# Raw weight pieces placed in the next chunk's tiles, a store cut in two, and loads moved to ScalarE's queue, in a kernel of attention, Fourier mixing and routed experts

## The chip, the cores and the metric

The kernel runs on one core of one Trainium2 chip. The metric is the device time of one launch in microseconds (us). Engines are TensorE (PE, with its weight loads as PEld), VectorE (DVE), ScalarE (ACT), GpSimd (POOL) and SyncE (SP); DMA issues of SP stand as SPq.

## The reference

Three stages follow each other, on four sequences of 576 tokens with 512 features, all in fp32: attention in a band of 128 with 8 heads of 64, a block of Fourier mixing with an MLP of 2048 hidden units, and a top-1 mixture of 8 experts with 1024 hidden units each.

```python
scores = np.where(mask, scores + bias[None], -1e9)      # mask: 0 <= query - key < 128
attn = softmax(scores); x = attn @ v                    # (4, 576, 512)
mixed = np.real(np.fft.fft(np.fft.fft(x, axis=1), axis=2))
u = x + mixed
un = (u - mean(u)) / np.sqrt(var(u) + 1e-06)
x = u + np.maximum(un @ w_ch1, 0.0) @ w_ch2
e = argmax(x @ w_gate)        # or the token before's expert, where sigmoid(x @ w_local) >= 0.5
out = p[e] * (np.maximum(x @ w1[e], 0.0) @ w2[e])       # p: softmax of the gate's logits
```

## The kernel before

Products that need fp32 accuracy are made as three matmuls (lines 162 to 164): each operand is split in a high and a low part of the fp32r type, a cast on ACT (L158) and a difference on DVE or POOL (L159). Tokens stand in 18 tiles of 128 rows, worked two at a time in nine groups.

**Attention** of one sequence goes in 20 steps, through scores (L330), mask, maximum, exponentials (L345), transposes (L354, L358) and values (L373). Its operands come in four *parts* a sequence, qk (642 KB) and v (384 KB), by `load_part` (L258 to L265) on SP's queue. A part is asked for at steps 0, 2 and 5 of the same sequence, into buffers that earlier parts must leave.

**Mixing** of one sequence multiplies by Fourier tables (L460 to L489) and stores u to DRAM (`ud`, L492 to L502). One of these stores (L493) takes rows 1 to 127 of a tile.

**The MLP's first half** (`mlp_first`, L595 on) uses 4 of 8 chunks of 256 hidden units for all nine groups, and leaves half sums y in `pd` (L612) and normalised, transposed tiles in `nd` (L579). The rows u of the next group are asked for (L553) at the sixth step of a group, and `normalise` goes on one stage a step from there: statistics on DVE (L558, L560), a chain of eleven small instructions on POOL (L565 to L573), scaling on ACT (L577), transposes on PE (L511). The first group takes its u from SBUF.

**Weights** of the MLP arrive as raw 64-bit numbers in 512 KB pieces, four a chunk. `convert` loads each piece into a ring of two buffers on SP's queue (L228), scales it on ACT (L232), and puts it together in three steps on DVE (L233 to L235) before the split of L158 and L159.

**Order.** `opening` (the first sequence's attention and mixing, the first chunk's conversion, the first group's normalise) is scheduled by hand. Then `run` interleaves lanes by planned positions: sequences 1 to 3, the conversions, and `mlp_first`. The MLP's second half adds both halves, routes the tokens and scatters their numbers into slots; `early` (L997) prepares the first tokens of the first expert meanwhile, whose weights `we` come by L940 on SP's queue; `slot_load` (L981) reads the slots back on the same queue. Eight experts end the kernel.

Each engine executes its instructions in order, and SP's DMA issues too: one that waits holds those behind it. `last` keeps instructions for `issue_after`, which lets a transfer start only after another was issued.

Of the kernel before, what the change touches and what calls it, by code (L numbers as in the profile page):

```python
# [13 lines left out]
I32 = mybir.dt.int32  # L14
# [11 lines left out]
FF = 4 * DM  # L26
# [28 lines left out]
FL = 2  # L55
EY = 8
EL = 7
HB = 4
VL = 3
NP = 5  # L60

QK = 2 * (HALF + 33)
# [88 lines left out]
def build(ctx, tc, a, out):  # L151
# [57 lines left out]

    def load_weights64(tiles, w1, w2, c, words):  # L210
        t1, t2 = tiles
        q = CB // 2
        for j in range(2):
            f0 = c * CB + j * q
            s = w1[:, 2 * f0:2 * (f0 + q)].rearrange("(k p) f -> p k f", p=P)
            convert(t1[:, 0, :, j * q:(j + 1) * q], t1[:, 1, :, j * q:(j + 1) * q], s, words)
            yield
        for j in range(CB // P):
            f0 = c * CB + j * P
            s = w2[f0:f0 + P].rearrange("p (k f) -> p k f", k=4)  # L220
            convert(t2[:, 0, j].rearrange("p (k f) -> p k f", k=4), t2[:, 1, j].rearrange("p (k f) -> p k f", k=4), s, words)
            yield

    def convert(hi, lo, src, words):

        k, n = hi.shape[1], hi.shape[2]
        r = wraw.tile([P, k, 2 * n], U32, tag="r64", name="r64", bufs=RB)
        nc.sync.dma_start(out=r, in_=src)  # L228
        w = r.rearrange("p k (n t) -> p k n t", t=2)
        wl, y = w[:, :, :, 0], w[:, :, :, 1]  # L230
        t = words().rearrange("p (k n) -> p k n", k=k)
# [25 lines left out]

    def load_part(b, g, part, pieces=1):  # L258

        t = qk.tile([P, 2, QK], F32, tag="qk", name="qkt")  # L260
        n = 2 // pieces
        for x in range(pieces):
            nc.sync.dma_start(out=t[:, x * n:(x + 1) * n], in_=a["qk"][b, g, part, :, x * n:(x + 1) * n])
        v = sm.tile([P, 3, 4 * D], F32, tag="v", name="vt", bufs=QB)
        last["load"] = nc.sync.dma_start(out=v, in_=a["v"][b, g, part].rearrange("p k h d -> p k (h d)"))  # L265
        return t, v

    raw0 = load_part(0, 0, 0, 2)

# [29 lines left out]
    def attention(b):  # L299
# [63 lines left out]
        def values(u):  # L363
# [18 lines left out]
            if i in (2, 4):  # L382
                R.pop((g, part))

        def natural(u):
# [18 lines left out]

        parts = [(g, p) for g in range(2) for p in range(2)]
        R[0, 0] = raw0 if b == 0 else load_part(b, 0, 0)
        ahead = 1
        for u in range(len(units) + VL + 1):
            if ahead < 4 and u in (0, 2, 5):
                g, p = parts[ahead]  # L410
                R[g, p] = load_part(b, g, p)
                ahead += 1
            if u < len(units):
                scores(u)
            if 1 <= u < len(units) + 1:
                exps(u - 1)
            yield
            if VL < u:
                natural(u - VL - 1)
            if FL <= u < len(units) + FL:  # L420
                flip(u - FL)
            if VL <= u < len(units) + VL:
                values(u - VL)
            yield

    def mixing(b):
# [44 lines left out]
        for kb in range(3):  # L471
# [19 lines left out]
            if kb == 0:  # L491
                nc.sync.dma_start(out=row(0), in_=xs[0][:, 0])  # L492
                nc.sync.dma_start(out=row(3)[1:P], in_=xs[0][1:P, 1])  # L493
            elif kb == 1:
                nc.sync.dma_start(out=row(1), in_=xs[1][:, 0])
                nc.sync.dma_start(out=row(2), in_=xs[1][:, 1])
            else:
# [3 lines left out]
                nc.sync.dma_start(out=um[r:r + 32], in_=xs[2][0:32, 0])  # L501
                nc.sync.dma_start(out=um[r + 32:r + 64], in_=xs[2][0:32, 1])  # L502
            if kb == 2:
# [42 lines left out]
    def normalise(gs, xT, us, src=None):  # L546
# [17 lines left out]
        v0, v1, v2 = (v[:, i, 0:n] for i in range(3))  # L564
        nc.gpsimd.tensor_scalar_add(v0, mv[:, 0:n, 1], 1.0e-6)  # L565
        nc.gpsimd.tensor_tensor(out=v1, in0=v0, in1=half[:, 0:n], op=ALU.pow)
        for _ in range(2):
            nc.gpsimd.tensor_tensor(out=v2, in0=v1, in1=v1, op=ALU.mult)
            nc.gpsimd.tensor_tensor(out=v2, in0=v2, in1=v0, op=ALU.mult)
            nc.gpsimd.tensor_scalar(out=v2, in0=v2, scalar1=-0.5, scalar2=1.5, op0=ALU.mult, op1=ALU.add)  # L570
            nc.gpsimd.tensor_tensor(out=v1, in0=v2, in1=v1, op=ALU.mult)
        nc.gpsimd.tensor_tensor(out=v2, in0=mv[:, 0:n, 0], in1=v1, op=ALU.mult)
        nc.gpsimd.tensor_scalar_mul(v2, v2, -1.0)  # L573
        yield
# [42 lines left out]
    chunksA = [weight_tiles(wpA) for c in range(FA // CB)]  # L617
    def tables():
# [5 lines left out]
    def setup():  # L624

        load = last["load"].ins
        with tc.issue_after(load):
# [8 lines left out]
    def conversions():  # L636
        for c in range(FA // CB):
            yield from load_weights64(chunksA[c], a["w_ch1"], a["w_ch2"], c, lambda: sm.tile([P, 2 * CB], U32, tag="t64", name="t64", bufs=2))

# [97 lines left out]
    lact = c2.enter_context(pool("lact", 2, reuse_waits="tile"))  # L737
    chunksB = [weight_tiles(wpB) for c in range(FA // CB, FF // CB)]

    room = lact.tile([P, 4, 2 * CB], U32, tag="xTe", name="t64", bufs=1)  # L740
    turns = iter(range(4 * FF // CB))
    for c in range(FA // CB, FF // CB):
        for _ in load_weights64(chunksB[c - FA // CB], a["w_ch1"], a["w_ch2"], c, lambda: room[:, next(turns) % 4]):
            pass
# [458 lines left out]
```

## Time and profile before

| | us |
|---|---|
| median of 3 runs (lowest to highest) | 1034.43 (1032.81 to 1038.68) |
| the profiled execution | 1039.1 |
| its span, first to last instruction | 1037.4 |
| PE busy | 946.8 (91%) |
| DVE, ACT, POOL busy | 520.1, 381.3, 241.1 |
| mean granted TensorE clock | 0.959 |

In what follows, a window's line gives busy time and instructions of each engine, then the granted clock as a share of the full one, the busy share of the 16 DMA engines (1 is all of them) and what they moved. A line of the timeline gives start, duration, engine, line, operation and tiles, and in brackets how long the engine had been idle and what ended that. A line of waits gives an engine's instruction, what it waited for, and the total, count and longest.

### The profile page before, as it was taken

The page shows a single profiled execution, that of the slowest core. Times are in us where ns is not written, and L with a number is a line of the kernel's source. Part 1 is how long each engine was busy: PE and PEld are TensorE (multiplying, and loading weights), DVE is VectorE, ACT ScalarE, POOL GpSimd, SP SyncE. Part 2 cuts the span into 40 slices and gives each one's busy share as a digit, 9 for nine tenths or more (in the row PEclk, how much of TensorE's full clock was granted, in tenths as well). Part 3 has the DMA queues.
Part 4 walks back from the last instruction along what each step waited for, and adds up shares of the span by engine and source line. Part 5 has one row for each costly group of instructions (what it writes and reads, how often), then busy time and mean ns, then how long its engine had stood idle before and what let it go on. Part 6 is the DMA issues. An engine that isn't in the chain of part 4 may idle for free. (4 is left out here: it accounts for less than half of the span.)

```text
span 1037.4 us, 16275 instructions
## 1 busy us (share of the span) xinstructions
PE 946.8 (91%) x5959; PEld 770.6 (74%) x5959; DVE 520.1 (50%) x1286; ACT 381.3 (37%) x990; POOL 241.1 (23%) x358
## 2 busy tenths in 40 slices
PE   8877989889799888899999999997987999999993
PEld 4636666567568567688988888886876988888993
DVE  5777856636444455611133535354767644555510
ACT  5345654353252233421111111112436644454510
POOL 2245531230222034401011222222122212111100
PEclk9987999899989998999999999999999999999997
DMA  8345841342212155514344444444349745555300
GB/s 301 98 128 158 283 153 43 131 140 69 78 36 63 57 188 166 184 61 102 62 102 102 103 102 102 103 102 122 123 144 302 237 142 183 179 163 183 119 18 18
DMA packets 112103, 133.58 MB, mean 129 GB/s; under 512 B 16253, under 2 KB 79998, under 8 KB 111950
## 3 DMA queue, kind: packets, MB, share of 16 engines
q1 hardware_dynamic: 89166, 112.73, 34.0%
q0 software_dynamic: 22848, 19.72, 8.8%
q8 instruction: 49, 0.80, 0.3%
q14 instruction: 40, 0.33, 0.1%
HBM read 104.08 MB, written 31.23 MB: 130 GB/s over the span
## 5 line engine op out<-in xcount | busy, mean ns | idle before, releaser
L527 ACT ACTIVATE h<-hps 128x256 fp32r<-128x256 f32 x152 | 58.1, 382 | 263.7 <-PE hps L164 257.9
L528 DVE SCALAR_TENSOR_TENSOR h<-hps,h 128x256 fp32r<-128x256 f32 x152 | 63.7, 419 | 173.8 <-ACT h L527 173.5
L162 PE MATMUL acc<-t,h 128*128 128x512 f32 x304 | 127.8, 423 | 7.9 <-ACT h L527 7.0
L163 PE MATMUL acc<-t,h 128*128 128x512 f32 x304 | 123.6, 407 | 0.9 <-POOL t L159 0.8
L164 PE MATMUL acc<-t,h 128*128 128x512 f32 x304 | 120.5, 400 | 0.5 <-DVE h L528 0.5
L159 DVE TENSOR_TENSOR t<-we,t 128x512 fp32r<-128x512 f32 x144 | 93.8, 686 | 53.0 <-ACT t L158 52.3
L158 ACT CAST t<-we 128x512 fp32r<-128x512 f32 x144 | 82.6, 618 | 49.7 <-PE acc L164 24.9
L162 PE MATMUL hps<-xT,t 128*128 128x256 f32 x288 | 87.9, 305 | 4.9 <-DVE h L528 2.8
L162 PE MATMUL hps<-xTe,t 128*128 128x256 f32 (+5 forms) x288 | 87.0, 303 | 2.3 <-ACT xTe L158 2.3
L163 PE MATMUL hps<-xTe,t 128*128 128x256 f32 (+5 forms) x288 | 86.7, 301 | 0.3 <-DVE xTe L159 0.3
L164 PE MATMUL hps<-xTe,t 128*128 128x256 f32 (+5 forms) x288 | 86.9, 302 | 0.0
L164 PE MATMUL hps<-xT,t 128*128 128x256 f32 x288 | 84.4, 293 | 0.2 <-POOL t L159 0.2
L163 PE MATMUL hps<-xT,t 128*128 128x256 f32 x288 | 84.1, 292 | 0.0
L162 PE MATMUL hps<-xTb,t 128*128 128x256 f32 x288 | 83.2, 289 | 0.0
L164 PE MATMUL hps<-xTb,t 128*128 128x256 f32 x288 | 82.6, 287 | 0.0
L163 PE MATMUL hps<-xTb,t 128*128 128x256 f32 x288 | 82.2, 286 | 0.0
L345 ACT ACTIVATE t<-t,mx 128x128 f32<-128x128 f32 (+1 forms) x160 | 62.6, 394 | 47.3 <-DVE mx L338 43.1
L162 PEld LDWEIGHTS acc<-t,h 128*128 128x128 f32 x304 | 58.1, 193 | 25.5 <-ACT h L527 11.9
L162 PEld LDWEIGHTS hps<-xT,t 128*128 128x128 f32 x288 | 57.6, 200 | 16.1 <-DVE h L528 7.6
L162 PE MATMUL acc<-t,hE 128*128 128x512 f32 x168 | 67.6, 402 | 0.1
L164 PEld LDWEIGHTS acc<-t,h 128*128 128x128 f32 x304 | 57.7, 191 | 12.6 <-DVE h L528 1.1
L163 PEld LDWEIGHTS acc<-t,h 128*128 128x128 f32 x304 | 58.8, 194 | 10.3 <-POOL t L159 2.3
(260 smaller groups left out, 2039.8 us busy)
## 6 DMA issues: line engine op xcount, KB each, us to landing
we<-in_w SPq DMA_DIRECT2D x72, 512.0 KB
r<-in_w_ch SPq DMA_DIRECT2D x32, 512.0 KB
qkt<-in_qk SPq DMA_DIRECT2D x15, 642.0 KB
nd<-xT SPq DMA_DIRECT2D x18, 512.0 KB
xTb<-nd POOLq DMA_DIRECT2D x18, 512.0 KB, 6.0
vt<-in_v SPq DMA_DIRECT2D x16, 384.0 KB
pd<-y SPq DMA_DIRECT2D x18, 256.0 KB
ub<-ud SPq DMA_DIRECT2D x18, 256.0 KB
```

Of the source, the lines that this page charges most:

```text
L158: nc.scalar.copy(hi, src)
L159: (eng or nc.vector).tensor_tensor(out=lo, in0=src, in1=hi.bitcast(F32), op=ALU.subtract)
L162: nc.tensor.matmul(o, lhsT=wh, rhs=xh, start=start, stop=False, **kw)
L163: nc.tensor.matmul(o, lhsT=wh, rhs=xl, start=False, stop=False, **kw)
L164: return nc.tensor.matmul(o, lhsT=wl, rhs=xh, start=False, stop=stop, **kw)
L345: nc.scalar.activation(t[0:m, j], t[0:m, j], AF.Exp, bias=mx[0:m, j:j + 1], scale=-1.0, accum_out=sums[0:m, j:j + 1])
L527: nc.scalar.activation(h[:, 0, 0:n], hps[:, 0:n], AF.Relu)
L528: nc.vector.scalar_tensor_tensor(out=h[:, 1, 0:n], in0=hps[:, 0:n], scalar=0.0, in1=h[:, 0, 0:n].bitcast(F32), op0=ALU.max, op1=ALU.subtract)
```

## The change

Seven things change. Raw pieces: those of chunk c (0 to 2, and 4 to 6) are loaded by `load_raw` into the tiles in which the next chunk's converted weights will stand, all at once, and chunks 3 and 7 alone use the ring. The 127-row store becomes one of 112 rows and one of 15. Parts from the fourth on are asked for by ACT's queue, three parts ahead, when a part is left. The half sums go to `pd` by ACT's queue. The first group's small chain runs on DVE, with a start value by integer arithmetic and three refinements (17 instructions) in place of POOL's power and two. The stages of `normalise` stand at steps 1, 5, 6, 9 and 11 of a group. In `early`, `slot_load` stands seven steps later and the wait ahead of the transposes is five steps instead of eight.

```diff
-EY = 8
+EY = 5
+STEPS = (1, 5, 6, 9, 11)
...
+    def load_raw(c, wp=None):
+
+        if wp is not None:
+            raws[c] = [x[:, i] for x in (wp.tile([P, 2, 4, CB], U32, tag=g, name="rw") for g in ("w1", "w2")) for i in range(2)]
+        for i, s in enumerate(blocks64(c)):
+            if wp is None:
+                raws.setdefault(c, []).append(wraw.tile([P, 4, CB], U32, tag="r64", name="r64", bufs=RB))
+            last["raw"] = nc.sync.dma_start(out=raws[c][i], in_=s)
+            yield
+
+    def load_weights64(chunks, i, c, wp, words):
+        t1, t2 = chunks[i] = weight_tiles(wp)
+        q = CB // 2
+        late_load = load_raw(c) if c not in raws else iter(())
...
-    def convert(hi, lo, src, words):
-
-        k, n = hi.shape[1], hi.shape[2]
-        r = wraw.tile([P, k, 2 * n], U32, tag="r64", name="r64", bufs=RB)
-        nc.sync.dma_start(out=r, in_=src)
+    def convert(hi, lo, r, words):
...
-    def load_part(b, g, part, pieces=1):
+    def load_part(b, g, part, pieces=1, eng=nc.sync):
...
             if i in (2, 4):
                 R.pop((g, part))
+                k = 4 * b + 2 * g + part + 3
+                if k < 4 * B:
+                    k = (k // 4, k % 4 // 2, k % 2)
+                    coming[k] = load_part(*k, eng=nc.scalar)
...
-        parts = [(g, p) for g in range(2) for p in range(2)]
-        R[0, 0] = raw0 if b == 0 else load_part(b, 0, 0)
-        ahead = 1
         for u in range(len(units) + VL + 1):
-            if ahead < 4 and u in (0, 2, 5):
-                g, p = parts[ahead]
-                R[g, p] = load_part(b, g, p)
-                ahead += 1
+            if b == 0 and u in (0, 2):
+                k = (0, u // 2, 1 - u // 2)
+                coming[k] = load_part(*k)
+            if u < len(units) and units[u][1] in (0, 3):
+                g, p = units[u][0], TILES[units[u][1]][0]
+                R[g, p] = coming.pop((b, g, p))
...
-                nc.sync.dma_start(out=row(3)[1:P], in_=xs[0][1:P, 1])
+
+                nc.sync.dma_start(out=row(3)[1:P - 15], in_=xs[0][1:P - 15, 1])
+                nc.sync.dma_start(out=row(3)[P - 15:P], in_=xs[0][P - 15:P, 1])
...
+        eng = nc.gpsimd if src is us else nc.vector
+        eng.tensor_scalar_add(v0, mv[:, 0:n, 1], 1.0e-6)
+        if src is us:
+            eng.tensor_tensor(out=v1, in0=v0, in1=half[:, 0:n], op=ALU.pow)
+        else:
+
+            r = v1.bitcast(I32)
+            eng.tensor_single_scalar(r, v0.bitcast(I32), 1, op=ALU.logical_shift_right)
+            eng.tensor_scalar(out=r, in0=r, scalar1=-1.0, scalar2=float(0x5F3759DF), op0=ALU.mult, op1=ALU.add)
+        for _ in range(2 if src is us else 3):
...
+            done = 0
             for n, _ in enumerate(ffn(xT, len(gs) * P, chunksA, (ps_h1,), acc, hidden, (ps_a, ps_a))):
-                if j + 1 < len(GA) and n >= NP:
-                    if pre is None:
+                if j + 1 < len(GA) and done < len(STEPS) and n >= STEPS[done]:
+                    if pre is None and (n >= NP or mixed[0] >= need[j + 1]):
                         yield ("need", lambda: mixed[0] >= need[j + 1])
                         pre = prepare(j + 1)
-                    next(pre, None)
+                    if pre is not None:
+                        next(pre)
+                        done += 1
...
-                nc.sync.dma_start(out=pd[g], in_=y)
+                nc.scalar.dma_start(out=pd[g], in_=y)
...
+            if n == 9:
+                for _ in load_raw(0, wpA):
+                    pass
+            if n == 14:
+                for c in range(1, nA - 1):
+                    for _ in load_raw(c, wpA):
+                        pass
...
+    with tc.issue_after(last["ud"].ins):
+        for c in range(nA, nA + nB - 1):
+            for _ in load_raw(c, wpB):
+                pass
...
+        for _ in range(EL):
+            yield
         x = slot_load(e * CAP, TM, 1)
-        for _ in range(EL):
+        for _ in range(2):
             yield
```

Three places show how instructions stand. The first is ACT's in-order queue in the opening, from the last transposed weights w of the first sequence's attention to the first copies of the mixing (r and rw are raw pieces, qkt and vt a part). Before:

```order
L358 COPY w<-pt 128x512 x2
L462 COPY z_723<-zps 128x289
L345 ACTIVATE t,sums<-t,mx 128x128
L462 COPY z_723<-zps 128x289
L462 COPY z_722<-zps 128x289
L232 ACTIVATE r_757<-r_757 128x512
L345 ACTIVATE t,sums<-t,mx 128x128 x5
L158 CAST t_229<-t_759 128x4x128
L462 COPY z_722<-zps 128x289
L462 COPY zn<-zps 1x289
L232 ACTIVATE r_776<-r_776 128x512
```

Now:

```order
L381 COPY w<-pt 128x512
L286 DMA qkt<-in_qk 128x1284
L288 DMA vt<-in_v 128x768
L381 COPY w<-pt 128x512
L286 DMA qkt<-in_qk 128x1284
L288 DMA vt<-in_v 128x768
L255 ACTIVATE rw<-rw 128x512 x8
L255 ACTIVATE r_1290<-r_1290 128x512
L255 ACTIVATE r_1292<-r_1292 128x512
L488 COPY z_745<-zps 128x289
L368 ACTIVATE t,sums<-t,mx 128x128
L488 COPY z_745<-zps 128x289
L488 COPY z_744<-zps 128x289
```

Two loads of a part now stand in ACT's queue, and ten scalings of raw pieces (two chunks and the ring) stand ahead of the mixing's first copy, where none stood.

The second is DVE from the statistics of the first group (st, mv) to the mixing's last sums (x, cmb). Before:

```order
L558 BN_STATS st<-x 128x6 x2
L560 BN_AGGR mv<-st 128x2
L334 COPY_PREDICATED s<-mask,s 65x4x65
L560 BN_AGGR mv<-st 128x2
L483 TENSOR_TENSOR cmb<-pc,cmb 33x257
L484 TENSOR_TENSOR cmb<-pc,cmb 33x257
L488 TENSOR_TENSOR x<-x,cmb 33x257
L489 TENSOR_TENSOR x<-x,cmb 33x255
L488 TENSOR_TENSOR x<-x,cmb 32x257
L489 TENSOR_TENSOR x<-x,cmb 32x255
```

Now:

```order
L586 BN_STATS st<-x 128x6 x2
L588 BN_AGGR mv<-st 128x2
L357 COPY_PREDICATED s<-mask,s 65x4x65
L588 BN_AGGR mv<-st 128x2
L359 SCALAR_TENSOR_TENSOR t<-s,bias 65x512
L595 TENSOR_SCALAR v<-mv 128x2
L361 TENSOR_REDUCE mx<-t 65x4
L601 TENSOR_SCALAR v<-v 128x2
L602 TENSOR_SCALAR v<-v 128x2
L604 TENSOR_TENSOR v<-v 128x2
L605 TENSOR_TENSOR v<-v 128x2
L606 TENSOR_SCALAR v<-v 128x2
```

The small instructions on v are new here; the seventeen of them (six are shown, the others follow) stand ahead of the last sums.

The third is SP's queue about the read of the first slots (ids), among the first expert's weight pieces (we), half sums read back (p_) and stores of x2d; ISA rows move no data. Before:

```order
L940 DMA we<-in_w 128x4x256
L940 ISA
L940 DMA we<-in_w 128x2x512
L1029 DMA p__6882<-pd_94 128x512
L1062 DMA x2d<-x_7156 128x512
L1029 DMA p__6887<-pd_95 128x512
L981 ISA
L981 DMA ids<-slots_115 128x2x4
L940 ISA
L940 DMA we<-in_w 128x4x256
```

Now:

```order
L990 DMA we<-in_w 128x4x256
L1081 DMA p__6884<-pd_95 128x512
L990 ISA
L990 DMA we<-in_w 128x2x512
L1114 DMA x2d<-x_7154 128x512
L990 ISA
L990 DMA we<-in_w 128x4x256
L1031 ISA
L1031 DMA ids<-slots_115 128x2x4
L990 ISA
L990 DMA we<-in_w 128x2x512
```

The read of ids stood behind two pieces of weights, and stands behind five; three more pieces were moved past it.

## Rows read from the trace of the kernel before

**Rows 1.** The span by windows: us, busy time (instructions) of each engine, PEclk, DMA share, GB/s

```profile
60.00:145.00 85.00, 69.25 (x410) 48.71 (x410) 64.50 (x121) 45.32 (x132) 43.81 (x61) 0.86 0.63 206
145.00:365.00 220.00, 200.30 (x1376) 148.25 (x1375) 109.79 (x260) 84.17 (x287) 42.44 (x109) 0.95 0.25 79
365.00:452.00 87.00, 74.03 (x407) 61.58 (x407) 48.46 (x86) 35.84 (x69) 31.71 (x52) 0.90 0.49 154
452.00:713.00 261.00, 257.79 (x1678) 226.09 (x1677) 94.94 (x347) 48.57 (x118) 51.23 (x48) 1.00 0.44 98
713.00:732.00 19.00, 12.48 (x71) 10.36 (x70) 8.20 (x31) 5.84 (x15) 5.67 (x5) 0.82 0.55 174
```

**Rows 2.** Shorter windows, with the same columns

```profile
10.00:15.00 5.00, 4.34 (x28) 2.24 (x24) 4.79 (x11) 3.46 (x17) 0.32 (x2) 1.00 1.02 412
70.00:75.00 5.00, 2.08 (x8) 1.27 (x8) 4.09 (x8) 1.39 (x5) 4.27 (x10) 0.50 0.86 257
190.00:213.00 23.00, 16.35 (x123) 12.18 (x121) 10.62 (x25) 9.81 (x35) 6.75 (x20) 0.85 0.31 108
275.00:295.00 20.00, 11.84 (x52) 6.40 (x52) 6.97 (x19) 4.29 (x15) 4.58 (x15) 0.66 0.18 60
275.00:280.00 5.00, 1.25 (x11) 1.01 (x10) 0.00 (x0) 0.00 (x0) 0.00 (x0) 1.00 0.06 25
285.00:290.00 5.00, 3.52 (x9) 0.84 (x7) 0.42 (x1) 4.29 (x15) 1.66 (x4) 0.50 0.18 64
437.00:445.00 8.00, 6.47 (x25) 5.82 (x26) 3.23 (x5) 3.45 (x7) 2.63 (x2) 0.57 0.00 0
```

**Rows 3.** The timeline about the third store of 127 rows

```profile
266.79 0.25 SPq L493 DMA_DIRECT2D ud<-x  x1
...
280.18 0.69 DVE L558 BATCH_NORM_STATS2 st<-u 128x6 f32<-128x512 f32 x1 [10.76 <-DMA u<-ud]
...
281.89 0.92 PE L373 MATMUL o<-w,vt 128*64 128x65 f32 x12 [5.64 <-DVE cmb L484]
```

**Rows 4.** The timeline of the first group's normalise

```profile
68.78 0.23 POOL L565 TENSOR_SCALAR v<-mv 128x2 f32<-128x2 f32 x1 [5.62 <-DVE mv L560]
...
75.20 0.24 POOL L573 TENSOR_SCALAR v<-v 128x2 f32<-128x2 f32 x1
...
76.34 0.48 PE L511 MATMUL tps<-ident,u 128*128 128x128 f32 x1 [2.56 <-ACT u L577]
```

**Rows 5.** What SP's DMA issues waited for: us in total, times, longest

```profile
SPq L612 <- ACT y L611: 86.3, 16, 22.3
SPq L228 <- DVE t L235: 81.7, 23, 13.1
...
SPq L263 <- PE s L330: 47.4, 9, 18.0
SPq L265 <- PE o L373: 35.3, 9, 7.8
```

**Rows 6.** What ACT waited for, with the same columns

```profile
ACT u L577 <- POOL v L573: 39.6, 9, 13.5
...
ACT r L232 <- DMA r<-in_w_ch: 15.3, 8, 3.3
```

**Rows 7.** The timeline of ACT before the mixing's first copy, and at a later group's normalise

```profile
53.98 0.40 ACT L462 COPY z<-zps 128x289 f32<-128x289 f32 x1 [12.40 <-PE zps L460]
...
436.69 1.52 ACT L577 ACTIVATE u<-u,v 128x512 f32<-128x512 f32 x2 [3.98 <-POOL v L573]
```

**Rows 8.** The timeline at the first expert

```profile
719.86 0.39 SPq L981 DMA_DIRECT2D ids<-slots  x1
...
722.05 0.17 DVE L990 CAST idn<-ids 128x4 uint32<-128x4 f32 x1 [5.80 <-DMA ids<-slots]
...
724.26 1.14 ACT L158 CAST t<-we 128x512 fp32r<-128x512 f32 x2 [9.10 <-DMA we<-in_w]
...
725.72 0.38 PE L795 MATMUL pn<-ident,lt 10*128 10x10 f32 x2 [6.43 <-ACT lt L791]
```

More of the change, by code (lines that the diff above doesn't have):

```diff
@@ L208, in weight_tiles, with blocks64 @@
         return (wp.tile([P, 2, 4, CB], F32R, tag="w1", name="t1"), wp.tile([P, 2, CB // P, DM], F32R, tag="w2", name="t2"))
-    def load_weights64(tiles, w1, w2, c, words):
-        t1, t2 = tiles
+    raws = {}
+    def blocks64(c):
+        w1, w2 = a["w_ch1"], a["w_ch2"]
         q = CB // 2
@@ L214, in load_weights64 @@
             f0 = c * CB + j * q
[L215 to L217 removed]
+            yield w1[:, 2 * f0:2 * (f0 + q)].rearrange("(k p) f -> p k f", p=P)
         for j in range(CB // P):
             f0 = c * CB + j * P
[L220 to L228 removed]
+            yield w2[f0:f0 + P].rearrange("p (k f) -> p k f", k=4)
+    def load_raw(c, wp=None):
[5 more added lines that the diff above has]
+            last["raw"] = nc.sync.dma_start(out=raws[c][i], in_=s)
+            yield
+    def load_weights64(chunks, i, c, wp, words):
+        t1, t2 = chunks[i] = weight_tiles(wp)
+        q = CB // 2
+        late_load = load_raw(c) if c not in raws else iter(())
+        for _ in range(RB - 1):
+            next(late_load, None)
+        for i in range(4):
+            next(late_load, None)
+            r = raws[c][i]
+            if i < 2:
+                convert(t1[:, 0, :, i * q:(i + 1) * q], t1[:, 1, :, i * q:(i + 1) * q], r, words)
+            else:
+                convert(t2[:, 0, i - 2].rearrange("p (k f) -> p k f", k=4), t2[:, 1, i - 2].rearrange("p (k f) -> p k f", k=4), r, words)
+            yield
+    def convert(hi, lo, r, words):
         w = r.rearrange("p k (n t) -> p k n t", t=2)
         wl, y = w[:, :, :, 0], w[:, :, :, 1]
[L231 removed]
+        t = words().rearrange("p (k n) -> p k n", k=4)
         nc.scalar.activation(y.bitcast(F32), y.bitcast(F32), AF.Copy, scale=BIAS)
@@ L262, in load_part @@
         for x in range(pieces):
-            nc.sync.dma_start(out=t[:, x * n:(x + 1) * n], in_=a["qk"][b, g, part, :, x * n:(x + 1) * n])
+            eng.dma_start(out=t[:, x * n:(x + 1) * n], in_=a["qk"][b, g, part, :, x * n:(x + 1) * n])
         v = sm.tile([P, 3, 4 * D], F32, tag="v", name="vt", bufs=QB)
-        last["load"] = nc.sync.dma_start(out=v, in_=a["v"][b, g, part].rearrange("p k h d -> p k (h d)"))
+        last["load"] = eng.dma_start(out=v, in_=a["v"][b, g, part].rearrange("p k h d -> p k (h d)"))
         return t, v
-    raw0 = load_part(0, 0, 0, 2)
+    coming = {(0, 0, 0): load_part(0, 0, 0, 2)}
     z16 = slab([P, 4 * P], BF16, "z16", "m", MB)
@@ L501, in mixing @@
                 nc.sync.dma_start(out=um[r:r + 32], in_=xs[2][0:32, 0])
-                nc.sync.dma_start(out=um[r + 32:r + 64], in_=xs[2][0:32, 1])
+                last["ud"] = nc.sync.dma_start(out=um[r + 32:r + 64], in_=xs[2][0:32, 1])
             if kb == 2:
@@ L564, in normalise @@
         v0, v1, v2 = (v[:, i, 0:n] for i in range(3))
[L565 to L573, printed above, removed]
+        eng = nc.gpsimd if src is us else nc.vector
+        eng.tensor_scalar_add(v0, mv[:, 0:n, 1], 1.0e-6)
+        if src is us:
+            eng.tensor_tensor(out=v1, in0=v0, in1=half[:, 0:n], op=ALU.pow)
+        else:
+            r = v1.bitcast(I32)
+            eng.tensor_single_scalar(r, v0.bitcast(I32), 1, op=ALU.logical_shift_right)
+            eng.tensor_scalar(out=r, in0=r, scalar1=-1.0, scalar2=float(0x5F3759DF), op0=ALU.mult, op1=ALU.add)
+        for _ in range(2 if src is us else 3):
+            eng.tensor_tensor(out=v2, in0=v1, in1=v1, op=ALU.mult)
+            eng.tensor_tensor(out=v2, in0=v2, in1=v0, op=ALU.mult)
+            eng.tensor_scalar(out=v2, in0=v2, scalar1=-0.5, scalar2=1.5, op0=ALU.mult, op1=ALU.add)
+            eng.tensor_tensor(out=v1, in0=v2, in1=v1, op=ALU.mult)
+        eng.tensor_tensor(out=v2, in0=mv[:, 0:n, 0], in1=v1, op=ALU.mult)
+        eng.tensor_scalar_mul(v2, v2, -1.0)
         yield
@@ L615, in mlp_first @@
                     yield ("piece", 0)
-    chunksA = [weight_tiles(wpA) for c in range(FA // CB)]
+    chunksA = [None] * nA
     def tables():
@@ L624, in setup @@
     def setup():
-        load = last["load"].ins
+        load = last["raw"].ins
         with tc.issue_after(load):
@@ L637, in conversions @@
         for c in range(FA // CB):
-            yield from load_weights64(chunksA[c], a["w_ch1"], a["w_ch2"], c, lambda: sm.tile([P, 2 * CB], U32, tag="t64", name="t64", bufs=2))
+            yield from load_weights64(chunksA, c, c, wpA, lambda: sm.tile([P, 2 * CB], U32, tag="t64", name="t64", bufs=2))
     END = object()
@@ L737, in build @@
     lact = c2.enter_context(pool("lact", 2, reuse_waits="tile"))
-    chunksB = [weight_tiles(wpB) for c in range(FA // CB, FF // CB)]
+    chunksB = [None] * nB
     room = lact.tile([P, 4, 2 * CB], U32, tag="xTe", name="t64", bufs=1)
     turns = iter(range(4 * FF // CB))
+    with tc.issue_after(last["ud"].ins):
+        for c in range(nA, nA + nB - 1):
+            for _ in load_raw(c, wpB):
+                pass
     for c in range(FA // CB, FF // CB):
-        for _ in load_weights64(chunksB[c - FA // CB], a["w_ch1"], a["w_ch2"], c, lambda: room[:, next(turns) % 4]):
+        for _ in load_weights64(chunksB, c - nA, c, wpB, lambda: room[:, next(turns) % 4]):
             pass
```

## The prediction, made before the changed kernel ran

> **What bounds the kernel now.** I read the windows first, with PE as the yardstick [rows 1]. From 452 to 713 us PE is busy 257.8 of 261 us: what is saved ahead of such a stretch comes off the end, since nothing there waits for anything but PE. So the time is to be had only where PE stands still or runs slowly, in four windows. 60 to 145: 69.25 of 85 busy, 15.8 idle. 145 to 365: 19.7 idle. 365 to 452: 13.0 idle. 713 to 732: 6.5 idle. Together 55.0 us.
>
> The granted clock is the second loss. In 70 to 75 and in 285 to 290 it is 0.50 [rows 2], the lower of its two levels (1.2 GHz); PE was busy 2.08 of 5 us in the first of these. With two levels, a mean of 0.86 over 85 us is 2 x 0.14 x 85 = 23.8 us at the lower one; the other three windows have 22.0, 17.4 and 6.8 us. The two rows have PE busy 5.60 of 10 us; at the full level that work would take half, so a us at the lower level costs about 0.28 us. That prices the four at 6.7, 6.2, 4.9 and 1.9. With idle time the change can reach 22.5 + 25.9 + 17.9 + 8.4 = 74.7 us at the very most.
>
> What ends the idle time came last. The third store of 127 rows is issued at 266.79, and statistics that need the rows u start at 280.18, after 10.76 us of waiting [rows 3]. Meanwhile the DMA engines are 0.06 busy, one of sixteen, and move 25 GB/s [rows 2]; 254 KB at 25 GB/s are 10.2 us. The first group's chain on POOL runs from 68.78 to 75.44, and PE has waited 2.56 us when its transposes start [rows 4].
>
> **The change part by part.** *The store in two.* Two stretches in 145 to 365 carry it: 275 to 295 has 8.2 us idle and 13.6 us at the lower clock (12.0 us by the price above), 190 to 213 has 6.7 and 6.9 (8.6 us) [rows 2]. That is 20.6 of the window's 25.9. If all sixteen engines take the 112 rows, 224 KB at the 412 GB/s seen elsewhere [rows 2] are 0.5 us in place of 10. The read of u stays, so I take four fifths, 16, and 2 more for the earlier steps of normalise elsewhere in this window: **-18**, from -11 to -25.
>
> The row shows one busy engine, not why. The Trainium skill, page "DMA: Bandwidth & Descriptors", section "Why a DMA increments its semaphore by 16 and not by 1", says that a transfer is given the largest number of engines up to 16 that divides its rows: 127 rows one, 112 sixteen, 15 fifteen; the trace agrees as far as its 0.06 goes.
>
> *60 to 145.* Seventeen small DVE instructions at 0.17 us [rows 8] (the nearest in size) are 2.9 us in place of POOL's 6.7, but DVE is busy 4.09 of 5 us there [rows 2] and takes its larger steps in between; I take 4.9, so -1.8 (0 to -3.8). Raw pieces that lie in place remove ACT's waits for them: 15.3 us over the kernel in 8 waits [rows 6], 1.9 each, one or two of them here: -2. The first store's cut, -2; the clock gives half of 6.7 back at best, -2. Sum **-8**, from -2 (only the chain) to -15 (two thirds of all that is there).
>
> *365 to 452.* The chain on POOL ends right ahead of ACT's scaling: 39.6 us of ACT's waits in nine, 3.98 of them at 436.69 [rows 6, 7], and 437 to 445 loses 1.5 idle and 1.9 by the clock [rows 2]. Three steps now stand between chain and scaling where one stood, so the wait is covered by a group's own matmuls. The weights of the second half come up to twelve pieces at once where SP stood 81.7 us for a free ring buffer [rows 5]. I take half of 17.9: **-9**, from -4 (this one stretch) to -16.
>
> *The first expert.* The read of ids at 719.86 waits for a scatter; the weights behind it come late, ACT's cast has waited 9.10 us for them, and PE 6.43 for ACT [rows 8]. With three more pieces ahead of that read, the cast finds its data. **-6.5**, from -3 (the read lands later, and DVE's 5.80 us wait for it becomes the next) to -8.4.
>
> *What is added.* The 26 loads of parts and 18 stores on ACT cost an issue each: 44 x 0.39 (an SP issue [rows 8]) = 17.2 us of an engine that is busy 84 of 220 and 36 of 87 us [rows 1]. SP's waits at these lines, 86.3 for y and 82.7 for PE [rows 5], mostly go: ACT makes y itself, and a load is placed where PE has done with the buffer. Behind an issue stand the activations h that PE waits for; I put a quarter on the path: **+4.3** (0 to +12). In the opening ten scalings stand ahead of a copy for which ACT stood 12.40 us [rows 7]; that idle time covers them unless the pieces land late. A part asked for behind eight pieces (4.2 MB at 412 GB/s, 10.2 us) may be late: **+2** (0 to +10), near the low end since parts are asked for three ahead. The new places of normalise and of the raw scalings can each make a stretch like 437 to 445 (3.4 us): none to three of them, **+5** (0 to +10). The two ends of waiting in `early` are one step apart and cost nothing while PE has work, as it does there.
>
> Sum: -8 - 18 - 9 - 6.5 = -41.5; +4.3 + 2 + 5 = +11.3; net -30.2. The profiled execution took 1039.1 (span 1037.4), so 1008.9; it lies 4.7 above the median of 1034.43, which makes the forecast **1004 us**. The distances of the terms to their ends, taken as independent (root of the squares), are 14 downward and 17 upward: 990 to 1021.
>
> **The rivals.** *The moved transfers come out dear.* ACT's issues, the opening and the new order all cost their upper end, 32 in place of 11.3: 1025. For it: ACT has not issued a DMA before, and no row shows one. Against: its busy shares above.
>
> *The cut does nothing.* The two pieces go through as slowly as the one, 16 us stay: 1020. The Trainium skill, same page, section "Rules for kernel authors", says that two transfers to disjoint halves of the partitions aren't worth it, as they use the same engines anyway. The 0.06 speaks against it here: the undivided store did not use them.
>
> *Slower: ACT held by its own queue.* ACT executes in order, and an issue that must wait, for PE's last read of the buffer or for an earlier transfer that used the same semaphore, holds the activations h behind it. The price is what SP bears at the two load lines, 82.7 us in 18 waits [rows 5]. If half of it comes to ACT with PE waiting: 1004 - 4.3 + 41.4 = 1041. It decides from 34.5 us, two fifths of these waits. For it: waits of up to 18.0 us. Against: SP stood early, having nothing else to do, and ACT comes to the place later.
>
> **How the numbers follow.** The forecast has 0.67, the dear transfers 0.13, the idle cut 0.12, the held queue 0.08. About 0.5%, 5 us, is what a measurement of this kernel tells from no change. Faster by more, under 1029: 0.65 + 0.09 + 0.11 = 0.85. Within: 0.02 + 0.04 + 0.01 = 0.07. Slower, 0.08. The range from 988 to 1028 leaves out 0.06 below it and 0.13 above (the held queue, and the worst of the dear case).
>
> **What would show it.** The cut: statistics at the third store start within some 5 us of it, and DMA share about the store is above 0.06. The clock about 190 to 213 and 275 to 295 is near 1. In 60 to 145 PE waits for its first transposes under 1 us. In 365 to 452 ACT's wait for POOL's chain is short. At the first expert ACT's cast no longer waits 9 us. Wrong would be: an ACT whose issues at the load lines last microseconds each, PE's wait for h above its present place, or a longer opening.

## The result

The changed kernel takes 1026.76 us (median of 9, 1024.84 to 1031.17) where the kernel before takes 1038.68 (median of 9 runs, the 3 shown above among them): a ratio of 0.9901, with a 95% interval from 0.9873 to 0.9929. It is faster, by 1.0%, where 2.9% were forecast (30 of 1034 us). The time lies inside the range of 988 to 1028, at its upper edge, but a third of the gain came. The profiled execution has a span of 1024.3 us.

The same windows as [rows 1], of the changed kernel:

```profile
60.00:145.00 85.00, 65.44 (x392) 47.54 (x391) 61.56 (x133) 38.36 (x110) 36.87 (x47) 0.84 0.40 128
145.00:365.00 220.00, 214.64 (x1494) 162.58 (x1493) 121.93 (x283) 93.21 (x314) 42.76 (x112) 0.98 0.32 98
365.00:452.00 87.00, 68.43 (x393) 57.66 (x392) 48.09 (x73) 33.04 (x65) 36.48 (x54) 0.92 0.46 144
452.00:713.00 261.00, 252.81 (x1629) 220.97 (x1628) 95.61 (x349) 48.65 (x118) 51.33 (x49) 0.99 0.43 94
713.00:732.00 19.00, 17.77 (x119) 15.60 (x119) 16.07 (x52) 8.74 (x19) 4.39 (x5) 1.00 0.53 168
```

From 145 to 365 PE is busy 214.6 us, where it was 200.3 [rows 1], and the granted clock is 0.98 in place of 0.95: the gain is there, about as forecast. From 60 to 145 it is 65.4 in place of 69.25. From 365 to 452, PE has 68.4 busy; before, 74.0. From 452 to 713 it has 252.8 and 257.8, and at the first expert, 713 to 732, 17.8 and 12.5. So part of the gain is lost again at either side. Windows at fixed times compare different work once a program has shifted; the starts of ACT's copies of the half sums mark nearly the same work in both. By the end of group 0 PE has made 792 matmuls in the changed kernel and 810 in the kernel before, so that mark favours it a little; by the end of group 1 it has made 1374 and 1372. The second copy of each group of two tiles starts at (us):

| end of group | 0 | 1 | 2 | 3 | 4 | 5 | 6 | 7 | 8 | span |
|---|---|---|---|---|---|---|---|---|---|---|
| before | 145.0 | 229.4 | 296.5 | 345.5 | 387.0 | 420.8 | 451.4 | 475.3 | 498.7 | 1037.4 |
| changed | 146.2 | 230.0 | 284.7 | 329.9 | 365.4 | 408.4 | 440.0 | 463.5 | 493.0 | 1024.3 |
| difference | +1.2 | +0.6 | -11.8 | -15.6 | -21.6 | -12.4 | -11.4 | -11.8 | -5.7 | -13.1 |

Two profiles whose engines execute the same orders that far (e3_cut_alone and f1_cut_early below) still differ by 2.5 us at the end of group 0 and by 1.1 at that of group 1, so differences of a us or two between single profiles say nothing. Groups 1 to 4 gain 22.8 us. Groups 5 to 8 give 15.9 back, in two places: group 5 (43.0 us in place of 33.8) and group 8 (29.5 in place of 23.4). The rest of the kernel gains 7.4. Three places of the changed kernel show where time went.

In the first group (timeline; start, duration, engine, line, operation):

```profile
75.07 0.17 DVE L609 TENSOR_SCALAR v<-v 128x2 f32<-128x2 f32 x1
...
78.39 0.69 DVE L258 SCALAR_TENSOR_TENSOR t<-rw,t 128x512 uint32<-128x512 uint32 x1
79.12 0.62 ACT L160 CAST t<-t 128x512 fp32r<-128x512 f32 x1 [5.79 <-DVE t L258]
79.64 0.81 ACT L613 ACTIVATE u<-x,v 128x512 f32<-128x512 f32 x1
...
80.50 1.12 PE L539 MATMUL tps<-ident,u 128*128 128x128 f32 x4 [7.45 <-ACT u L613]
```

The chain on DVE ends at 75.24, where POOL's ended at 75.44 [rows 4]. ACT could scale u then, but a cast of converted weights stands ahead of it in ACT's order, and DVE makes that weight's last step (L258) only after the chain and after the mixing's sums. PE waits 7.45 us, 2.56 before.

Some 20 us later, on POOL and PE:

```profile
96.10 1.71 POOL L161 TENSOR_TENSOR t<-t,t 128x512 fp32r<-128x512 f32 x1
...
97.89 0.46 POOL L595 TENSOR_SCALAR v<-mv 128x2 f32<-128x2 f32 x1
...
102.18 0.24 POOL L609 TENSOR_SCALAR v<-v 128x2 f32<-128x2 f32 x1
102.39 1.27 POOL L161 TENSOR_TENSOR t<-t,t 128x512 fp32r<-128x512 f32 x1
...
103.72 0.79 PE L165 MATMUL acc<-t,h 128*128 128x512 f32 x1 [5.51 <-POOL t L161]
```

POOL's chain for the second group stands between two differences of weights (L161), and PE waits 5.51 us for the second. It does so with the old steps of normalise as well (4.0 us, e4_old_steps below), and not with the new steps where no pieces lie ahead (0.8 us at the longest, f8_cut_early_steps_parts).

At the end of the first half:

```profile
460.67 2.10 POOL L1079 DMA_DIRECT2D xTb<-nd  x2 [12.46 <-PE hps L166]
...
469.08 0.55 PE L164 MATMUL hps<-xTb,t 128*128 128x256 f32 x1 [4.56 <-DMA xTb<-nd]
```

And the window from 460 to 480, with the columns of [rows 1]:

```profile
460.00:480.00 20.00, 15.44 (x84) 13.39 (x84) 2.12 (x5) 3.09 (x7) 2.10 (x2) 0.83 0.40 79
```

PE takes one matmul of the MLP's second half (its operand is xTb) between two of group 8 (the early matmul, below), and waits 4.56 us for the tile to be loaded. In PE's order it stands 133 rows ahead of the others of its kind. Rows of the built program, PE, changed kernel:

```
L166 MATMUL hps<-xT,t_779 128x256
L164 MATMUL hps<-xTb,t_4699 128x256
L164 MATMUL acc<-t_780,h 128x512
```

Over those 20 us the granted clock is 0.83; with its two levels that makes 6.8 us at the lower one. Group 8 took 6 us more.

### The profile page after: what moved, and what is told of

Read it like the earlier page. It is cut to its first block, busy times and chain, and to the rows that moved or that the text cites. A ratio compares the mean times of both kernels' runs of the same rounds, so it can differ in the third digit from the quotient of the medians.

```text
span 1024.3 us, 16230 instructions
## 1 busy us (share of the span) xinstructions
PE 939.8 (92%) x5958; PEld 770.2 (75%) x5959; DVE 526.1 (51%) x1303; ACT 381.8 (37%) x990; POOL 235.2 (23%) x346
## 5 line engine op out<-in xcount | busy, mean ns | idle before, releaser
L161 DVE TENSOR_TENSOR t<-we,t 128x512 fp32r<-128x512 f32 x144 | 95.1, 695 | 55.8 <-ACT t L160 52.4
L164 PE MATMUL hps<-xTe,t 128*128 128x256 f32 (+5 forms) x288 | 88.0, 306 | 2.9 <-ACT xTe L160 2.9
L166 PE MATMUL hps<-xTe,t 128*128 128x256 f32 (+5 forms) x288 | 87.7, 305 | 0.0
L165 PE MATMUL hps<-xTe,t 128*128 128x256 f32 (+5 forms) x288 | 87.6, 304 | 0.0
L165 PE MATMUL hps<-xTb,t 128*128 128x256 f32 x288 | 81.7, 284 | 0.0
L164 PE MATMUL acc<-t,hE 128*128 128x512 f32 x168 | 66.9, 398 | 0.0
```

Source lines behind the costliest of these rows:

```text
L161: (eng or nc.vector).tensor_tensor(out=lo, in0=src, in1=hi.bitcast(F32), op=ALU.subtract)
L164: nc.tensor.matmul(o, lhsT=wh, rhs=xh, start=start, stop=False, **kw)
L165: nc.tensor.matmul(o, lhsT=wh, rhs=xl, start=False, stop=False, **kw)
L166: return nc.tensor.matmul(o, lhsT=wl, rhs=xh, start=False, stop=stop, **kw)
```

## The experiments

Each part was put on the kernel before, alone or beside the cut, or taken out of the changed one. Ratios are against the kernel before, on the same chip.

**The cut alone** (e3_cut_alone), on the kernel before:

```diff
-                nc.sync.dma_start(out=row(3)[1:P], in_=xs[0][1:P, 1])
+                nc.sync.dma_start(out=row(3)[1:P - 15], in_=xs[0][1:P - 15, 1])
+                nc.sync.dma_start(out=row(3)[P - 15:P], in_=xs[0][P - 15:P, 1])
```

> The kernel before with the store of 127 rows as one of 112 and one of 15, and nothing else. Theory: this alone carries the gain between 145 and 365 us: 16 to 22 us faster than before, with the DMA engines no longer at 0.06 after the store. Rival: the gain there came from loads of parts on ACT's queue or from rows asked for sooner, and the cut gives under 8.

0.9798 (0.9756 to 0.9840), 1015.8 us: the cut alone is faster than the whole change, by 1% of the kernel. At the third store of the cut kernel:

```profile
257.57 0.33 SPq L493 DMA_DIRECT2D ud<-x  x1
...
257.94 0.46 SPq L494 DMA_DIRECT2D ud<-x  x1
...
259.01 0.34 SPq L554 DMA_DIRECT2D u<-ud  x1
...
261.78 0.69 DVE L559 BATCH_NORM_STATS2 st<-u 128x6 f32<-128x512 f32 x1 [1.58 <-DMA u<-ud]
```

The statistics start 4.2 us after the store's issue, 13.4 before [rows 3], and wait 1.58 us in place of 10.76. Between issue and statistics (257.6 to 261.8) the DMA share is 0.54. At the end of group 4 the cut kernel is as far as the changed one: 365.6 us against 365.4, 387.0 before. It has gained 4.3 of that by the end of group 0, and groups 1 to 4 take 224.9 us in place of 242.0. So the cut alone accounts for the whole lead at that point, and the other parts together cost about 10 us by the end of the kernel (1015.8 to 1026.8; by the ratios, 0.0103).

**The chain back on POOL** (e1_pool_norm), in the changed kernel:

```diff
-        eng = nc.gpsimd if src is us else nc.vector
+        eng = nc.gpsimd
```

> The changed kernel with the first group's small chain back on POOL. Theory: on DVE the chain pushes back the last sums and the weights' conversion; ACT's cast of these weights stands ahead of its scaling of u, so PE's transposes start later (80.5 us, where 76.3 was before). On POOL they start near 77 again and the kernel is 2 to 5 us faster than the changed one. Rival: the lateness comes from the pieces already lying in SBUF, and the chain's engine doesn't matter: within 1 us of the changed kernel, with transposes still past 79.

0.9887 (0.9859 to 0.9916), against 0.9901 of the changed kernel: within the intervals. The transposes do start earlier, at 77.8 instead of 80.5, but group 0 ends only 1.0 us earlier (145.2), which is within what two profiles differ by, and the end does not move. The expected 2 to 5 us weren't there.

**The ring for chunks 4 to 6** (e2_ring_second), in the changed kernel:

```diff
-    with tc.issue_after(last["ud"].ins):
-        for c in range(nA, nA + nB - 1):
-            for _ in load_raw(c, wpB):
-                pass
```

> The changed kernel with chunks 4 to 6 loaded through the ring of two again, as before; chunks 0 to 2 as changed. Theory: twelve pieces at once let their conversions crowd 356 to 390, where DVE is 37.9 of 50 us busy and PE waits for the activations h; the ring spreads them, DVE falls to about 28 of 50, and the kernel is 8 to 14 us faster than the changed one. Rival: the later loss comes from the stages of normalise at their new steps; then within 2 us of the changed kernel.

0.9857 (0.9815 to 0.9899): 2.6 to 4.6 us faster (by medians and by ratios), a third of what was expected. The mechanism is in the trace, though. The window from 360 to 410, with the columns of [rows 1], in turn of the kernel before, of the changed kernel, and of the one with the ring:

```profile
360.00:410.00 50.00, 41.49 (x229) 34.15 (x229) 27.65 (x57) 18.92 (x37) 16.37 (x32) 0.90 0.56 175
```

```profile
360.00:410.00 50.00, 36.67 (x199) 30.26 (x197) 37.87 (x58) 22.94 (x44) 24.95 (x36) 0.90 0.54 171
```

```profile
360.00:410.00 50.00, 39.91 (x223) 33.52 (x222) 32.25 (x55) 22.74 (x43) 20.50 (x34) 0.90 0.64 193
```

DVE is busy 27.7 of 50 us before, 37.9 with all pieces there (the expectation's 37.9 is of this window) and 32.3 with the ring, so it fell by about half of what was expected; PE 41.5, 36.7 and 39.9. The DMA engines are no busier with all pieces there (0.54, against 0.56 and 0.64), so it is not their traffic. With twelve pieces in place nothing paces their conversions, and they stand ahead of the second step of the activations h, on DVE:

```profile
387.33 1.28 DVE L257 SCALAR_TENSOR_TENSOR t<-rw,t 128x512 uint32<-128x512 uint32 x2
388.53 0.68 DVE L258 SCALAR_TENSOR_TENSOR t<-rw,t 128x512 uint32<-128x512 uint32 x1
389.14 0.41 DVE L556 SCALAR_TENSOR_TENSOR h<-hps,h 128x256 fp32r<-128x256 f32 x1
...
389.60 0.39 PE L164 MATMUL hps<-xT,t 128*128 128x256 f32 x1 [2.33 <-DVE h L556]
```

PE's wait for that step over the whole kernel, in total, times and longest, in turn of the kernel before, of the changed kernel, and of the one with the ring:

```profile
PE hps L162 <- DVE h L528: 2.8, 4, 0.9
```

```profile
PE hps L164 <- DVE h L556: 6.4, 5, 2.3
```

```profile
PE hps L164 <- DVE h L556: 1.9, 3, 0.8
```

The kernel before has some of these waits too; 3.6 us more of them came with the pieces, and 4.5 went with the ring. Groups 5 to 8 take 121.1 us with the ring, 127.6 without.

**The old steps** (e4_old_steps), in the changed kernel:

```diff
-STEPS = (1, 5, 6, 9, 11)
+STEPS = (5, 6, 7, 8, 9)
```

> The changed kernel with the stages of normalise at steps 5, 6, 7, 8 and 9 as before. Theory: the new steps take ACT's wait for POOL's chain away in some groups, so this is 3 to 8 us slower than the changed kernel. Rival: the new steps cause the losses after 365 us; then it is 5 us or more faster.

0.9861 (0.9823 to 0.9899): 3 to 4 us faster, if anything. Neither expectation held: neither slower nor 5 us faster. In the changed kernel the new steps are no gain, though the intervals overlap.

Since three single undoings had not found the loss, the parts were then added one by one to the cut.

**The cut and slot_load** (f1_cut_early): the cut, and in `early`

```diff
-EY = 8
+EY = 5
...
+        for _ in range(EL):
+            yield
         x = slot_load(e * CAP, TM, 1)
-        for _ in range(EL):
+        for _ in range(2):
```

> The kernel before with the store cut and with the new place of slot_load in early, nothing else. Theory: the two gains lie in different stages and add, 21 us for the cut and 6 to 7 for the read of ids: about 1009, 26 to 29 under before. Rival: with the cut, the first expert's stall has gone or been covered already, and nothing is added: 1016.

0.9763 (0.9715 to 0.9812), 1013.2: 2.6 to 3.6 us on top of the cut, half of the expected 6 to 7 (the intervals overlap, so even that is not certain). With the cut alone PE's wait for ACT at the first expert is 2.88 us, 6.43 before [rows 8]: half of that stall had already gone.

**The cut and raw pieces ahead** (f2_cut_raw): the cut, `load_raw`, and its loops in the opening and ahead of the second half, as in the change.

> The kernel before with the store cut and with raw pieces loaded ahead into the next chunk's tiles, nothing else. Theory: the pieces in place let conversions crowd the opening's end and the stretch after mixing 3; slower than the cut alone (1015.8) by 4 to 12 us, after 365 us above all. Rival: the pieces are harmless alone (the ring brought back in the second half gave only 2 us), within 2 us of the cut alone.

0.9871 (0.9822 to 0.9921), 1025.6: 8 to 10 us slower than the cut alone, as the theory had it. Two places: the first statistics start at 73.7 us (67.2 with the cut alone), and groups 5 to 8 take 121.7 us (111.1). The first does not stand in the changed kernel, where they start at 68.5. Here the parts are on SP's queue behind the raw pieces, and from 40 to 50 us PE runs at a granted clock of 0.50, with the cut alone at 1.00; how the one leads to the other is not shown.

**The cut, parts and half sums on ACT's queue** (f3_cut_parts):

```diff
+                    coming[k] = load_part(*k, eng=nc.scalar)
...
-                nc.sync.dma_start(out=pd[g], in_=y)
+                nc.scalar.dma_start(out=pd[g], in_=y)
```

> The kernel before with the store cut, parts of queries, keys and values on ACT's queue three ahead, and half sums stored by ACT's queue. Theory: this brings PE's order in which one matmul of the second half stands 133 rows early and waits 4 to 5 us for its tile; with ACT's issues the whole is 5 to 9 us slower than the cut alone. Rival: ACT's issues cost nothing and the parts come sooner: the same as the cut alone or up to 4 us faster.

0.9860 (0.9790 to 0.9930), 1025.5: 6 to 10 us slower than the cut alone, as expected, though its four runs spread from 1016.3 to 1028.7 and the interval reaches that of the cut alone. The early matmul is there and waits 4.61 us.

**The cut and the new steps** (f4_cut_steps):

```diff
+STEPS = (1, 5, 6, 9, 11)
...
-                if j + 1 < len(GA) and n >= NP:
+                if j + 1 < len(GA) and done < len(STEPS) and n >= STEPS[done]:
```

> The kernel before with the store cut and with the stages of normalise at steps 1, 5, 6, 9 and 11, nothing else. Theory, after the old steps made the changed kernel 3 us faster: the later scaling and transposes come in the way of the activations h; 2 to 5 us slower than the cut alone. Rival: it takes ACT's waits for POOL's chain away as meant, 3 to 6 us faster.

0.9766 (0.9717 to 0.9815), 1014.2: 1.6 to 3.3 us faster than the cut alone, if anything; the expected 2 to 5 us slower is not there. Without the crowd of conversions the new steps may gain about what they cost with it; both differences are within the intervals.

**Half sums or parts** (f6_cut_pd, f7_cut_partsonly): each half of f3_cut_parts by itself.

```diff
-                nc.sync.dma_start(out=pd[g], in_=y)
+                nc.scalar.dma_start(out=pd[g], in_=y)
```

> The kernel before with the store cut and the half sums stored by ACT's queue, nothing else. In the built program one matmul of the second half then stands 133 rows early in PE's order. Theory: PE waits 4 to 5 us there and falls to the lower clock after: the last group of the first half is 6 us longer, 1020 to 1023. Rival: the 18 issues themselves hold ACT, spread over all groups.

0.9842 (0.9794 to 0.9891), 1023.1: 4.6 to 7.3 us slower than the cut alone. In its trace:

```profile
462.57 0.55 PE L162 MATMUL hps<-xTb,t 128*128 128x256 f32 x1 [4.87 <-DMA xTb<-nd]
```

Group 8 takes 29.8 us, 23.4 with the cut alone; the way from group 0's end to group 4's takes 225.3 and 224.9. So the loss does not lie where the stores are spread, about half of the 18 issues among those groups (0.33 us each), but in the one group with the early matmul.

```diff
+                    coming[k] = load_part(*k, eng=nc.scalar)
```

> The kernel before with the store cut and the parts asked for by ACT's queue three ahead, nothing else; PE's order has no early matmul. Theory: the 26 issues on ACT cost 0 to 4 us against the cut alone, 1014 to 1020. Rival: ACT's queue holds the activations, 1022 or more; in the first sequence PE would wait for s and for h more often.

0.9780 (0.9732 to 0.9828), 1015.6: the same as the cut alone. Twenty-six loads on ACT's queue cost nothing that these runs can tell. The issues in ns, least, median and most:

```profile
L263 ACTq DMA_DIRECT2D qkt<-in_qk x13: 334/335/380, 22.6 to 239.7; - x13
L265 ACTq DMA_DIRECT2D vt<-in_v x13: 334/334/2026, 23.1 to 266.1; - x13
```

One of them took 2.03 us; the others stayed under 0.4.

**Both undone** (e11_two_undone): the changed kernel with half sums on SP's queue and the ring for chunks 4 to 6.

```diff
-                nc.scalar.dma_start(out=pd[g], in_=y)
+                nc.sync.dma_start(out=pd[g], in_=y)
...
-    with tc.issue_after(last["ud"].ins):
-        for c in range(nA, nA + nB - 1):
-            for _ in load_raw(c, wpB):
-                pass
```

> The changed kernel with half sums back on SP's queue (no early matmul in PE's order) and chunks 4 to 6 through the ring. Theory: these two are the loss after 365 us (6 and 8 to 10 us): 1009 to 1015, the stretch from group 5 to the end of group 8 near 113 us as with the cut alone. Rival: the new steps or ACT's loads hold the loss: 1018 or more.

0.9768 (0.9720 to 0.9815), 1014.5: 12 to 14 us faster than the changed kernel. The end of group 4 to that of group 8 takes 113.0 us, where the changed kernel has 127.6, the cut alone 111.1 and the kernel before 111.7. The loss after 365 is these two parts.

**Half sums undone alone** (e6_pd_sp): the changed kernel with

```diff
-                nc.scalar.dma_start(out=pd[g], in_=y)
+                nc.sync.dma_start(out=pd[g], in_=y)
```

> The changed kernel with the half sums back on SP's queue; PE's order then has no early matmul. Theory: 5 to 7 us faster than the changed kernel (1020), and the last group of the first half takes 23.4 us again, not 29.5; what crowds the conversions stays, so 365 to the end of that group stays 4 us or more longer than with the cut alone. Rival: with the early matmul gone the crowding costs nothing, 1013 to 1016.

0.9832 (0.9799 to 0.9865), 1018.8: 7 to 8 us faster than the changed kernel, group 8 at 23.4 us again, and the way from group 4 to group 8 at 118.3. The four corners by ratio are 0.9901 (both), 0.9857 (ring), 0.9832 (half sums back), 0.9768 (both undone): 0.0044 and 0.0069 singly, 0.0133 together, so they add, within the intervals.

**The chain undone as well** (e12_three_undone): e11_two_undone with the chain back on POOL.

> The changed kernel with half sums on SP's queue, chunks 4 to 6 through the ring and the first group's chain on POOL; what is left is the cut, slot_load, the steps, the parts on ACT and chunks 0 to 2 ahead. Theory: the DVE chain costs 1 to 3 us in the first group, so 1011 to 1014 against 1014.5 with it. Rival: no difference, since the earlier transposes end in later waits of the same stretch.

0.9767 (0.9731 to 0.9803), 1010.4, against 0.9768: no difference by ratio, though transposes start at 78.3 and not at 79.7. The chain's engine makes no difference that these runs can measure.

**Everything but raw pieces, half sums and chain** (f8_cut_early_steps_parts): the kernel before with cut, `slot_load`, steps and parts.

> The kernel before with the cut, slot_load, the steps and the parts on ACT's queue, without raw pieces ahead. Theory: chunks 0 to 2 ahead gain nothing between 60 and 145 us, where the first group's conversions now come together and DVE is full: as fast as the kernel without raw and chain changes, 1009 to 1013, and not slower than the one with chunks 0 to 2 ahead. Rival: the pieces ahead carry a gain of 2 us or more there, and this is that much slower.

0.9736 (0.9701 to 0.9771), 1008.8: the fastest of all, and 0.0031 under e12_three_undone, from which it differs by chunks 0 to 2 in the ring. The intervals overlap; the traces agree with the sign:

```profile
60.00:145.00 85.00, 72.97 (x469) 52.48 (x470) 63.67 (x123) 49.85 (x143) 46.46 (x65) 0.92 0.61 191
```

PE is busy 73.0 of 85 us from 60 to 145 without pieces ahead, and 67.9 with them (e12_three_undone); the wait of PE for POOL's difference, 5.5 us there, is 0.8 at the longest here in that stretch. Group 1 ends at 221.3 us here and at 225.9 there.

**Without parts too** (f5_cut_early_steps): cut, `slot_load` and steps.

> The kernel before with the store cut, the new place of slot_load and the new steps of normalise, without raw pieces ahead, ACT's queue or the DVE chain. Theory: parts add, 1015.8 for the cut, 2.6 less by slot_load and 1.6 less by the steps, as measured one by one: 1010 to 1013 and the fastest so far. Rival: the steps and the cut remove the same waits, and it is no better than cut and slot_load (1013).

0.9749 (0.9701 to 0.9796), 1012.5, within the expected 1010 to 1013. That fits gains that add, but the rival's 1013 (no better than cut and `slot_load`) lies as near, and the intervals do not tell them apart.

## Why the prediction was wrong, point by point

**What bounds the kernel** was read rightly: the time came from idle PE and low clock in the named windows, and what the cut saved ahead of 365 reached the end.

**The store in two** was right in place and mechanism; its term with the steps was -18, and with the cut alone the kernel is 21 us faster, 17.1 of them in groups 1 to 4 and 4.3 ahead of these, where 2 were put. The signs named came in part: the statistics start 4.2 us after the store, the DMA share is 0.54, and the clock from 275 to 295 is 1.00 in the changed kernel; from 190 to 213 it is 0.93, 0.85 before. The slow store behind the low DMA share [rows 2] was the cause, and both rules of the Trainium skill named there were put to the test: the one from "DMA: Bandwidth & Descriptors", section "Why a DMA increments its semaphore by 16 and not by 1", holds in its consequence (10.76 us of waiting became 1.58); that of "Rules for kernel authors", that two transfers to disjoint halves of the partitions aren't worth it, does not fit a store of 127 rows, whose cut made the kernel 2.0% faster.

**60 to 145** was forecast at -8 and came out at +1.2 (end of group 0) or +0.6 (end of group 1, where the counts of matmuls agree). The cut alone is 4.3 us ahead at the end of group 0 and 9.2 at the end of group 1 (220.2 us), so its own part here, put at -2, was larger, and the other parts lost more than it gave. The failing step was the gain by raw pieces in place, put at -2. ACT's waits for pieces went as forecast (15.3 us in the kernel before, 5.0 in the changed one), but conversions that had been spread by the ring now come together with the second group's chain on POOL (PE's 5.51 us): chunks 0 to 2 ahead end group 1 by 4.6 us later (e12_three_undone against f8_cut_early_steps_parts) and cost about 3 us at the end of the kernel, within the intervals. The new steps of normalise end group 1 by 3 to 7 us later (226.7 us in f4_cut_steps against 220.2, 224.1 in f5_cut_early_steps against 221.3 in f1_cut_early, 230.0 in the changed kernel against 224.0 in e4_old_steps); no term of the forecast had that, and they win it back by the end of group 4. The price of the chain on DVE was a second failing step, with little weight. I priced its instructions (2.9 to 4.9 us; it took 4.4, and started 2.0 us later) and not what stands behind them on DVE: sums and a conversion whose cast stands ahead of u on ACT, so that PE waited 7.45 us where under 1 was forecast. Undoing it alone brought nothing, so the chain is worth nothing measurable in either direction.

**365 to 452** was forecast at -9, and 15.9 us were lost to the end of group 8. The failing step: I read SP's 81.7 us of waiting for a ring buffer [rows 5] as a cost. It paced the conversions: DVE was busy 27.7 of the 50 us from 360 to 410 before, and 37.9 after. A wait of SP that PE did not wait for was booked as a gain; PE's wait for DVE's step of h, named as a sign of being wrong, rose from 2.8 to 6.4 us instead. Lifting it cost 4.6 to 6.6 us by the ratios (ring back in the changed kernel, alone and after half sums; by the medians 2.6 to 4.3). The steps of normalise, the other part of this term, gained 1.6 to 3.3 us where the conversions don't crowd, and lost about as much where they do, both within the intervals. That a group's own matmuls would cover ACT's wait for POOL's chain failed: the wait fell from 39.6 [rows 6] to 32.4 us, but the cut alone has 29.4 already (the longest wait, 13.5 us at the third store, is gone with it), and the changed kernel with the old steps has 27.8. In seven of the eight groups ACT still stands ready when the chain ends. Why is open.

**The first expert** was forecast at -6.5; the stages after group 8 gained 7.4 in the changed kernel, but slot_load alone on the cut gave 2.6 to 3.6. The cut had taken half of the stall (PE's wait 2.88 us in place of 6.43), in a part of the kernel that it does not touch. ACT's cast waits 3.99 us in the changed kernel, 9.10 before [rows 8]:

```profile
705.86 1.14 ACT L160 CAST t<-we 128x512 fp32r<-128x512 f32 x2 [3.99 <-DMA we<-in_w]
```

**What was added.** ACT's issues were put at +4.3, with a rival at 1041 in which ACT's queue holds. Both were the wrong mechanism: parts on ACT cost nothing measurable (f7_cut_partsonly) and no issue on ACT's queue in the changed kernel lasted over 0.4 us. The stores of half sums cost 5 to 8 us, and the loss lies where an instruction order changed with them: one matmul moved by 133 rows. The built program shows the order; the prediction rests on the orders of ACT, DVE and SP at the places of the change, and not on PE's, far from it. The term for new stretches by order, +5 (0 to +10), stood for such a thing and was too small: the early matmul (about 7) and the pieces ahead (about 3 and 7 in the two halves) make some 17 by the ratios.

**The opening** was put at +2 and measured +1.5 (first statistics at 68.5, 66.9 before). PE waited 1.0 us for a part, and ACT 1.8 for a piece. That fits the term, but profiles of kernels with the old opening start them at 66.7 to 67.8, so most of the +1.5 is within what profiles differ by.

**The rivals.** The dear transfers, 1025, came nearest by the number, but not for its reasons. The idle cut and the held queue are refuted.

Put together by the runs, in units of 0.001 of the time: the cut -20.2, slot_load -3.5, steps -3.2, parts -1.8, chain 0, chunks 0 to 2 ahead +3.1, chunks 4 to 6 ahead +6.4, half sums on ACT +6.9. The sum is -12.3, the whole -9.9, which agree within the intervals. Clear of the intervals are the cut, half sums on ACT, and the last two together (13.3); chunks 4 to 6 by themselves nearly so, and slot_load, steps, parts and chunks 0 to 2 not.

What stays open is why the order of PE changes with the engine of a store: the scheduler's reason isn't in any trace. Nor was a kernel run in which the early matmul alone was moved back, so that its order is the cause rests on the place of the loss: group 8 takes 27.8 to 31.2 us in all six kernels that have it (the changed one, e1, e2, e4, f3 and f6) and 23.4 in those without.

## What to carry to other kernels

When a trace shows a transfer that leaves the DMA share at 0.06 for 10 us and PE waiting behind it, mend that first, alone, and measure it: here one line is worth twice the seven changes together. A queue that waits for a ring buffer can pace the work behind it, so before lifting the limit ask which engine will then get that work in one piece, and what stands behind it in that engine's order. And after any change of an engine or a queue compare PE's order of the whole program, also far from the change: here a store's queue was changed, and the loss of 5 to 8 us lay about one matmul 133 rows early, on an engine that the store does not use.

## What the runs showed of the hardware that was not expected

A DMA issue on ACT's queue lasts 0.33 us in the changed kernel (26 loads of parts, 18 stores; the longest 0.40), as the same stores did on SP's queue before (0.33). A rare one is longer: 2.03 us for one load of f7_cut_partsonly. Small DVE instructions on 128 x 2 elements last 0.16 us but follow each other by 0.20 (timeline of the changed kernel, 71.51 to 75.07 us), so seventeen need 3.4 us, and two larger ones came in between.
